# Folding the first modulation into the QKV weights of a fused adaLN, windowed-attention and GEGLU kernel

## The chip, the cores and the metric

One NeuronCore of a Trainium2 chip runs the whole kernel. Its engines run side by side, each through an instruction list of its own: TensorE (PE, with PEld for its weight loads), VectorE (DVE), ScalarE (ACT), GpSimd (POOL) and SyncE (SP), which here issues nearly all DMAs. They wait for each other through semaphores. The metric is the device time of one execution in microseconds (us).

## The reference

`x` has 2048 rows of 512; all matrices are bf16. `c` is one conditioning row, from which six vectors of 512 are made.

```python
mod = (silu(c) @ w_mod).reshape(1, 6, 1, -1)          # sa, ca, ga, sb, cb, gb
h = layernorm(x) * (1 + ca) + sa
q, k, v = split(h @ wqkv)                             # 32 heads of 16
logits = einsum(q, k at positions s, s-2, ..., s-14) * 16 ** -0.5
o = softmax(logits) @ (v at the same 8 positions)
x = x + ga * (o @ wo)
h = layernorm(x) * (1 + cb) + sb
x = x + gb * ((gelu(h @ w_gate) * (h @ w_up)) @ w_down)      # inner size 1792
```

Since the modulation acts on the columns of the normalised row `xn`, `h @ wqkv = xn @ (diag(1 + ca) wqkv) + sa @ wqkv`.

## The kernel before, in words

The rows are cut into four groups of 512 (`sg` 0 to 3), each of four chunks of 128 rows. For each group the kernel does the following:

- The first layernorm (`norm`, `norm_act`): DVE takes statistics (`bn_stats`, L394) of some chunks, ACT of the others (L377, L383), POOL raises the variance to the power -0.5 (L425), and DVE writes the normalised rows `xn` (L434).
- A transposition to `hT` (columns on partitions). Group 0 is transposed by PE in halves (`transp0`, L471). Groups 1 and 2 are transposed by PE, 16 matmuls of 128x128 against the identity (`transp`, L448), and ACT applies `1 + ca` and `sa` while it copies the result out of PSUM (`transp_ev`, L486). Group 3 is transposed by one DMA of SP (L454), and ACT applies the modulation in place.
- The projections (`qkv`, L553): twelve units of four 128x512 matmuls, one for each of q, k, v and each quarter `j` of the columns. ACT copies each out of PSUM (`qkv_ev`, L567 to L571). The PSUM pool `mm` has four buffers, so that a unit waits until the unit four places earlier has been copied out.
- The logits: DVE multiplies q with eight shifted views of k (`pq`, L616, 128x4096 elements, four for each group; group sg's are called pq sg.0 to sg.3 here), and PE sums over the 16 elements of a head with a 0/1 matrix (`LTp`, L630, 8 matmuls that use 32 columns of the array each, for each `pq`). A softmax on DVE and ACT follows.
- The values: `v` is stored to DRAM (`vscr`, L590) and loaded back in windows (`V`, L598). Its tile `vT` has one buffer; POOL copies the last 16 columns of the group before into its head (`vhalo`, L579, from `vh`, L586). DVE multiplies with the probabilities (`pv`, L705), PE sums (`o_ps`, L719), then the output projection (`x_ps`, L740) and the residual (L749). `pq` and `pv` share four buffers (`prod`).
- The second layernorm of the group, and the gated FFN: `g_ps` and `u_ps` (L770) and `y_ps` (L782).

The vectors ga, sb, cb, gb are made by PE (`gR_ps`, L343) and taken through DRAM. Fifteen matmuls on zeros (L202) at the start keep PE running before there is work.

The order of the instructions on all engines is written out by hand: every generator below is a thread, the list `ORDER` names the thread whose next operation is issued, and each engine works through its operations in that order, without overtaking. The numbers with which `Op` objects are made (0.865 and the like) don't set anything on the chip.

Of the kernel before, what the change touches and what calls it, by code (L numbers as in the profile page):

```python
# [104 lines left out]
def kernel(  # L105
# [798 lines left out]
```

## Time and profile before

| | |
|---|---|
| median of 3 runs | 235.75 us (235.43 to 236.03) |
| the profiled execution's own time | 235.66 us |
| its span, first to last instruction | 233.9 us |
| PE busy | 229.1 us, 1382 matmuls |
| DVE busy | 168.2 us |
| ACT busy | 152.5 us |
| POOL busy | 24.3 us |
| granted TensorE clock, mean | 1.000 |

The span lies 1.8 us below the execution's own time, which also holds what goes before the first and after the last instruction. A view by time (the timeline) gives start and duration of merged instructions; in brackets stands how long the engine had been idle, and who released it. Neighbouring instructions of an engine overlap at their ends, so that the distance between starts, and not the printed duration, is what one more instruction costs an engine in a dense stretch. The chain of waits follows the last instruction back to what it waited for.

### The profile page before, as it was taken

To read this page: it belongs to the slowest core of one execution; us is meant where nothing else is said; L and a number is where in the kernel's file an instruction comes from. 1 tells how busy PE (TensorE), PEld (TensorE's weight loads), DVE (VectorE), ACT (ScalarE), POOL (GpSimd) and SP (SyncE) were. 2 spreads that over 40 slices of the span, in tenths; PEclk is the share of its full clock that TensorE was granted. 3 is DMA by queue.
4 is the path that set the end of the run, shared out by engine and by line. 5 is a ranking of instruction groups with operands and counts; after the bars stand their busy time and mean duration, and the time that the engine had idled before them with its cause. 6 is when DMAs were issued, how large, how long until landed. Compare 5 with 4: busy or idle time off the path is not lost.

```text
span 233.9 us, 3653 instructions
## 1 busy us (share of the span) xinstructions
PE 229.1 (98%) x1382; PEld 106.9 (46%) x1382; DVE 168.2 (72%) x240; ACT 152.5 (65%) x284; POOL 24.3 (10%) x37
## 2 busy tenths in 40 slices
PE   7899999999999999999999999999999999999995
PEld 2755454444544344444444444444444444444443
DVE  4889999999998999999899996944852213222222
ACT  4999998877997579936786961634468631467400
POOL 3210320791200000100000010000100000000000
PEclk9999999999999999999999999999999999999999
DMA  6999776999188582045003616110023000100011
GB/s 212 386 348 241 218 301 154 266 367 396 41 266 227 209 291 82 1 92 157 22 0 100 273 45 122 38 45 0 0 47 69 0 22 22 44 4 0 0 48 45
DMA packets 30217, 30.42 MB, mean 130 GB/s; under 512 B 14840, under 2 KB 26104, under 8 KB 30200
## 3 DMA queue, kind: packets, MB, share of 16 engines
q1 hardware_dynamic: 29664, 29.67, 40.8%
q10 hardware_dynamic: 536, 0.53, 0.6%
q8 instruction: 11, 0.18, 0.3%
q14 instruction: 6, 0.05, 0.1%
HBM read 22.78 MB, written 5.31 MB: 120 GB/s over the span
## 4 chain that ended last, share of the span: by engine, by line
PE 84%; DVE 9%; DMA 3%; ACT 1%; SPq 1%; issue 0%
PE g_ps L770 21%; PE u_ps L770 21%; PE y_ps L782 19%; PE qkv_ps L553 9%; PE x_ps L740 6%; DVE pq L616 5%; PE o_ps L719 3%; DMA x<-in_A_x_dram 3%; PE LTp L630 2%; PE y_ps L793 1%; DVE xn L434 1%; DVE st L394 1%; ACT qT L567 1%; DVE e L674 1%; DVE LTp L653 1%; DVE mx L647 1%
## 5 line engine op out<-in xcount | busy, mean ns | idle before, releaser
L770 PE MATMUL g_ps<-h,Wg 128*128 128x512 bf16 x224 | 57.5, 379 | 0.0
L770 PE MATMUL u_ps<-h,Wu 128*128 128x512 bf16 x224 | 57.5, 379 | 0.0
L820 DVE TENSOR_TENSOR hht<-gl,ub 128x512 bf16<-128x512 bf16 x56 | 23.0, 420 | 33.7 <-ACT ub L809 33.5
L782 PE MATMUL y_ps<-Wd,hht 128*128 128x512 bf16 x210 | 47.0, 379 | 0.0
L809 ACT CAST ub<-u_ps 128x512 bf16<-128x512 f32 x56 | 32.9, 588 | 20.4 <-PE u_ps L770 20.4
L802 ACT ACTIVATE gl<-g_ps 128x512 bf16<-128x512 f32 x56 | 33.6, 600 | 18.4 <-PE g_ps L770 16.9
L553 PE MATMUL qkv_ps<-hT,wqkv 128*128 128x512 bf16 x184 | 42.2, 380 | 0.0
L616 DVE TENSOR_TENSOR pq<-qT,kT 128x4096 bf16<-128x4096 bf16 x16 | 36.2, 2282 | 0.6 <-ACT kT L569 0.3
L705 DVE TENSOR_TENSOR pv<-PT,V 128x4096 bf16<-128x4096 bf16 x16 | 35.8, 2282 | 0.0
L770 PEld LDWEIGHTS <-Wu 128*128 128x128 bf16 x224 | 21.7, 98 | 27.0 <-issue 1.3
L770 PEld LDWEIGHTS <-Wg 128*128 128x128 bf16 x224 | 21.7, 98 | 27.0 <-issue 1.3
L782 PEld LDWEIGHTS <-hht 128*128 128x128 bf16 x210 | 20.4, 98 | 25.0 <-issue 0.4
L553 PEld LDWEIGHTS <-wqkv 128*128 128x128 bf16 x184 | 20.1, 114 | 18.5 <-issue 2.3
L425 POOL TENSOR_TENSOR rstd<-rstd,neghalf 128x4 f32<-128x4 f32 (+1 forms) x9 | 8.7, 971 | 124.4 <-DVE rstd L414 74.7
L827 DVE TENSOR_TENSOR ot<-y_ps,x 128x512 bf16<-128x512 f32 x15 | 10.1, 686 | 13.2 <-PE y_ps L782 13.2
L749 DVE TENSOR_TENSOR x<-x_ps,x 128x512 bf16<-128x512 f32 x16 | 10.7, 684 | 6.9 <-PE x_ps L740 6.9
L740 PE MATMUL x_ps<-woP,oT 128*128 128x512 bf16 x64 | 15.3, 379 | 0.0
L730 ACT CAST oT<-o_ps 128x512 bf16<-128x512 f32 x16 | 9.2, 593 | 8.7 <-PE o_ps L719 8.7
L394 DVE BATCH_NORM_STATS2 st<-x 128x6 f32<-128x512 bf16 x19 | 12.6, 680 | 2.7 <-DMA x<-in_A_x_dram 2.6
L486 ACT ACTIVATE h<-h,modT,scl 128x512 bf16<-128x512 bf16 x12 | 9.0, 809 | 7.7 <-DMA h<-xn 7.7
L586 POOL COPY vh<-vT 128x64 bf16<-128x64 bf16 x3 | 11.7, 3899 | 14.5 <-ACT vT L571 14.5
L377 ACT ACTIVATE gl<-x 128x512 bf16<-128x512 bf16 x13 | 8.3, 645 | 4.7 <-DVE x L749 3.0
(78 smaller groups left out, 189.6 us busy)
## 6 DMA issues: line engine op xcount, KB each, us to landing
V<-vscr SPq DMA_DIRECT2D x16, 526.0 KB, 6.8
wm<-in_w_mod_dram SPq DMA_DIRECT2D x5, 512.0 KB, 8.6
vscr<-vT SPq DMA_DIRECT2D x4, 528.0 KB, 9.5
out_dram<-ot SPq DMA_DIRECT2D x15, 128.0 KB, 1.7
Wg<-in_B_w_gate_dram SPq DMA_DIRECT2D x1, 1792.0 KB
Wu<-in_B_w_up_dram SPq DMA_DIRECT2D x1, 1792.0 KB
wqkv<-in_A_wqkv_dram SPq DMA_DIRECT2D x3, 512.0 KB, 7.3
x<-in_A_x_dram SPq DMA_DIRECT2D x3, 512.0 KB, 7.4
```

Source lines behind the costliest of these rows:

```text
L394: nc.vector.bn_stats(out=k["st", c4][:], in_=src()[:, c4, :])
L553: nc.tensor.matmul(ps[:], lhsT=wqkv[blk][:, dt, j::4], rhs=B["hT", sg][:, :, dt, :], start=(dt == 0), stop=(dt == DT - 1))
L586: yield Op("POOL", 0.2, lambda: nc.gpsimd.tensor_copy(out=vh[:], in_=B["vT", sg][:, :, SG:VR]), after=[f"qkv.{sg}.2.3"], fire=f"vh.{sg}")
L616: nc.vector.tensor_tensor(out=pq[:], in0=_ap(B["qT", sg][:, j, :], [[0, W], [1, SG]]), in1=_ap(kT[:, j, sg * SG + 2:sg * SG + 2 + SG], [[2 ...
L705: nc.vector.tensor_tensor(out=t[:], in0=_ap(B["PT", sg][:, 0, :], [[SG, 2], [0, 4], [1, SG]]), in1=_ap(v[:, j, 0, :], [[8, 2], [VR, 4], [1 ...
L740: nc.tensor.matmul(ps[:], lhsT=B["oT", sg][:, j, c4 * P:(c4 + 1) * P], rhs=woP[:, j, :], start=(j == 0), stop=(j == 3))
L749: nc.vector.tensor_tensor(out=x[:, c4, :], in0=B["x1ps", sg, c4][:], in1=x[:, c4, :], op=ALU.add)
L770: nc.tensor.matmul(ps[:], lhsT=Wt[:, dt, ft * P:(ft + 1) * P], rhs=B["h2T", sg][:, :, dt, :], start=(dt == 0), stop=(dt == DT - 1))
L782: nc.tensor.matmul(ps[:], lhsT=B["hh", sg, ft][:, c4 * P:(c4 + 1) * P], rhs=B["Wd", ft // 4][:, ft % 4, :], start=(ft == 0), stop=(ft == F ...
L802: nc.scalar.activation(out=gl[:], in_=B["g", sg, ft][:], func=ACT.Gelu_apprx_tanh)
L809: nc.scalar.copy(out=ub[:], in_=B["u", sg, ft][:])
L820: nc.vector.tensor_tensor(out=hh[:], in0=B["gl", sg, ft][:], in1=B["ub", sg, ft][:], op=ALU.mult)
```

## The change

The shift and scale of the first modulation leave the row side for groups 1 to 3.

- Twelve scaled weight tiles `wq` of 128x512 are made: `wqkv` times `1 + ca`, which is a scalar on each partition. POOL makes eight (all four of q, two of k, two of v), ACT four (`WENG`). They lie in twelve of the sixteen buffers `hh` that later hold the FFN's products.
- The shift becomes a bias `sa @ wqkv`: 48 matmuls on PE of 128 columns each (`bR_ps`, L382, of the same shape as `gR_ps`), one copy by ACT (L388), a store to DRAM and a load `bC` (L392, L396). ACT adds it while it copies the projections of groups 1 to 3 out of PSUM (L623), now with an ACTIVATE of function Identity in place of a CAST.
- Groups 1 to 3 are transposed by DMA (L502). The 32 PE transposes and the 12 ACT modulations of these groups go.
- Group 0 keeps its old path and the plain weights.
- The loads of `w_down` wait for the bias and the scaled weights, and no longer for the projections of all groups.
- `ORDER` is another list.

```diff
+    WENG = {(0, 0): "POOL", (0, 1): "POOL", (0, 2): "POOL", (0, 3): "POOL", (1, 0): "POOL", (1, 1): "POOL",
+            (1, 2): "ACT", (1, 3): "ACT", (2, 0): "POOL", (2, 1): "POOL", (2, 2): "ACT", (2, 3): "ACT"}
+
+    def wqscale(eng):
...
+                    if eng == "ACT":
+                        nc.scalar.activation(out=w[:], in_=wqkv[blk][:, dt, :], func=ACT.Copy, scale=scl[:, dt:dt + 1])
+                    else:
+                        e = nc.gpsimd if eng == "POOL" else nc.vector
+                        e.tensor_scalar_mul(out=w[:], in0=wqkv[blk][:, dt, :], scalar1=scl[:, dt:dt + 1])
+                yield Op(eng, 0.6, f, after=[f"wqkv{blk}", "mod1"], fire=f"wq.{blk}.{dt}")
+
+    def qkv_bias():
...
+            for blk in range(3):
+                for kt in range(4):
+                    for ch in range(4):
+                        nc.tensor.matmul(ps[H * ch:H * ch + H, blk, :], lhsT=B["shB"][:, kt, :],
+                                         rhs=wqkv[blk][:, kt, ch * P:(ch + 1) * P],
+                                         start=(kt == 0), stop=(kt == 3), tile_position=(0, H * ch))
...
+            nc.sync.dma_start(out=bscr.rearrange("b (c n) -> c b n", n=P), in_=B["bS"][0:P:H, :, :])
...
+            nc.sync.dma_start(out=bC[:], in_=bass.AP(bscr.tensor, bscr.offset, [[4, P], [D, 3], [1, 4]]))
...
-    BY_PE = ("LN1.1", "LN1.2", "LN2.0")
+    BY_PE = ("LN2.0",)
...
-                    nc.tensor.matmul(ps[:], lhsT=wqkv[blk][:, dt, j::4], rhs=B["hT", sg][:, :, dt, :],
+                    w = B["wq", blk, dt] if sg else wqkv[blk][:, dt, :]
+                    nc.tensor.matmul(ps[:], lhsT=w[:, j::4], rhs=B["hT", sg][:, :, dt, :],
...
+                if sg:
+                    nc.scalar.activation(out=o, in_=ps[:], func=ACT.Identity, bias=bC[:, blk, j:j + 1])
+                else:
+                    nc.scalar.copy(out=o, in_=ps[:])
...
-                     ... ("h1", lambda q: ln1_ev(q) if q else ln1_ev0(False)), ("qkv", qkv),
+                     ... ("h1", lambda q: iter(()) if q else ln1_ev0(False)), ("qkv", qkv),
```

What the order does to the engines is shown at three places. On PE, whose rows are long runs of equal instructions, it is told in words. Before: PE ran the ten last units of group 0's projections, with the 16 transposes of group 1 between them, then LTp 0.0, `gR_ps`, LTp 0.1, three units of group 1, LTp 0.2, LTp 0.3. Now: the same ten units, with the 48 bias matmuls after the second of them, LTp 0.0 ahead of the last, then LTp 0.1, `gR_ps`, LTp 0.2, two units of group 1, LTp 0.3, `gR_ps`, and then 19 units of groups 1 and 2 in one piece. The changes between 32-column matmuls and full ones number the same in the whole program (16 runs of 32-column matmuls before and now).

SP, before, from the load of the last group of `x` (`vscr` is the store of `v`, `V` its load in windows, `gB` the vector ga, `escr` the softmax's probabilities):

```order
L216 DMA x<-in_A_x_dram 128x4x512
L590 DMA vscr_108<-vT 128x2112
L223 DMA wm<-in_w_mod_dram 128x4x512
L297 DMA gscr_112<-gR 4x128
L598 DMA V_563<-vscr_108 128x1x2104
L302 DMA gB<-gscr_112 128x512
L598 DMA V_563<-vscr_108 128x1x2104 x2
L590 DMA vscr_109<-vT 128x2112
L297 DMA gscr_113<-gR 4x128
L686 DMA escr_116<-e 128x1024
```

SP, now, behind that load, the store of the bias and one load of `wm`:

```order
L502 DMA_TRANSPOSE hT<-xn 128x16x128
L396 DMA bC<-bscr 128x3x4
L225 DMA wm<-in_w_mod_dram 128x4x512
L644 DMA vscr_108<-vT 128x2112
L299 DMA gscr_112<-gR 4x128
L225 DMA wm<-in_w_mod_dram 128x4x512
L652 DMA V_664<-vscr_108 128x1x2104 x2
L502 DMA_TRANSPOSE hT<-xn 128x16x128
L299 DMA gscr_113<-gR 4x128
L740 DMA escr_117<-e 128x1024
L644 DMA vscr_109<-vT 128x2112
L304 DMA gB<-gscr_112 128x512
```

The two transpositions, which wait for `xn` of groups 1 and 2, stand ahead of the stores of `v` of groups 0 and 1 and of the loads of `V`; group 1's store (`vscr_109`) has moved behind the store of the probabilities of group 0 (`escr`), and the load of `gB` behind both.

POOL, before, from the powers of group 0's layernorm to that of group 2's:

```order
L425 TENSOR_TENSOR rstd<-rstd,neghalf 128x2 x2
L425 TENSOR_TENSOR rstd<-rstd,neghalf 128x4
L586 COPY vh<-vT 128x64
L579 COPY vT<-vh 128x4x16
L425 TENSOR_TENSOR rstd<-rstd,neghalf 128x4
```

POOL, now, in the same stretch:

```order
L473 TENSOR_TENSOR rstd<-rstd,neghalf 128x2 x2
L367 TENSOR_SCALAR wq<-wqkv_137,scl 128x512 x2
L196 MEMSET kT 128x4x16
L367 TENSOR_SCALAR wq<-wqkv_137,scl 128x512 x2
L367 TENSOR_SCALAR wq<-wqkv_138,scl 128x512
L473 TENSOR_TENSOR rstd<-rstd,neghalf 128x4
L367 TENSOR_SCALAR wq<-wqkv_138,scl 128x512
L367 TENSOR_SCALAR wq<-wqkv_139,scl 128x512 x2
L640 COPY vh<-vT 128x64
L473 TENSOR_TENSOR rstd<-rstd,neghalf 128x4
L633 COPY vT<-vh 128x4x16
```

Eight scaled tiles stand around the power of group 1's layernorm, and the clearing of the first columns of `kT`, which pq 0.0 reads, has moved behind two of them.

DVE, before, from pq 0.0 to pq 0.3:

```order
L616 TENSOR_TENSOR pq<-qT,kT 128x4096
L434 TENSOR_SCALAR xn<-x,mv,rstd 128x512
L394 BN_STATS st<-x 128x6
L434 TENSOR_SCALAR xn<-x,mv,rstd 128x512 x2
L434 TENSOR_SCALAR xn<-x,sums,rstd 128x512
L616 TENSOR_TENSOR pq<-qT,kT 128x4096
L394 BN_STATS st<-x 128x6
L616 TENSOR_TENSOR pq<-qT,kT 128x4096 x2
```

DVE, now, over the same instructions:

```order
L670 TENSOR_TENSOR pq<-qT,kT 128x4096
L442 BN_STATS st<-x 128x6
L482 TENSOR_SCALAR xn<-x,mv,rstd 128x512
L442 BN_STATS st<-x 128x6
L482 TENSOR_SCALAR xn<-x,mv,rstd 128x512 x2
L482 TENSOR_SCALAR xn<-x,sums,rstd 128x512
L670 TENSOR_TENSOR pq<-qT,kT 128x4096 x2
L448 BN_AGGR mv<-st 128x2 x2
L670 TENSOR_TENSOR pq<-qT,kT 128x4096
```

One `BN_STATS` has moved ahead of the `xn` of group 1, and two `BN_AGGR` ahead of pq 0.3; the sum of DVE's work is the same.

More of the change, by code (lines that the diff above doesn't have):

```diff
@@ L275, in ffn_q @@
             for b in range(4):
[L276 removed]
+                yield Op("SP", 0.65, ldwd(b), fire=f"Wd{b}", lat=mb(0.5 if b < 3 else 0.25), after=[f"qp.0.{blk}.3" for blk in range(3)] + ["mpb"] + [f"wq.{blk}.{dt}" for blk in range(3) for dt in range(DT)])
         return act_q(), sp_q(), wm_q(), ffn_q()
@@ new lines, in qkv_bias, with f @@
+    def qkv_bias():
+        def f():
+            B["shB"] = T("hh", [P, 4, H], BF16, "shB")
+            nc.scalar.copy(out=B["shB"][:], in_=_ap(modT[:, 0:4], [[1, 4], [0, H]]))
+        yield Op("ACT", 0.25, f, after=["mod0"], take=[SL["hh"]], fire="shB")
+        def f():
+            ps = T("mm", [P, 3, P], F32, "bR_ps")
+            B["bR"] = ps
+            for blk in range(3):
+                for kt in range(4):
[3 more added lines that the diff above has]
+                                         start=(kt == 0), stop=(kt == 3), tile_position=(0, H * ch))
+        yield Op("PE", 0.64, f, quad=True, after=["shB", "wqkv0", "wqkv1", "wqkv2"], take=[SL["mm"]], give=[SL["hh"]], fire="mpb")
+        def f():
+            B["bS"] = T("ot4", [P, 3, P], F32, "bR")
+            nc.scalar.copy(out=B["bS"][:], in_=B["bR"][:])
+        yield Op("ACT", 0.4, f, after=["mpb"], take=[SL["ot4"]], give=[SL["mm"]], fire="gcb")
+        def f():
+            nc.sync.dma_start(out=bscr.rearrange("b (c n) -> c b n", n=P), in_=B["bS"][0:P:H, :, :])
+        yield Op("SP", 0.65, f, after=["gcb"], give=[SL["ot4"]], fire="bst", lat=0.3)
+        def f():
+            nc.sync.dma_start(out=bC[:], in_=bass.AP(bscr.tensor, bscr.offset, [[4, P], [D, 3], [1, 4]]))
+        yield Op("SP", 0.65, f, after=["bst"], fire="bC", lat=0.5)
@@ L556, in qkv @@
             tk = [SL["q"]] if (blk, j) == (0, 0) else []
-            yield Op("PE", 0.865, f, after=[f"LN1.{sg}.h{d}" for d in (("0.1", "1.0", "3.1") if sg == 0 else (2, 3))] + [f"wqkv{blk}"], take=[SL["mm"]] + tk,
-                     give=[SL["hT"]] if last else [], fire=f"qp.{sg}.{blk}.{j}")
+            yield Op("PE", 0.865, f, after=([f"LN1.0.h{d}" for d in ("0.1", "1.0", "3.1")] + [f"wqkv{blk}"]
+                                               if sg == 0 else [f"LN1.{sg}.t"] + [f"wq.{blk}.{dt}" for dt in range(DT)]),
+                     take=[SL["mm"]] + tk, give=[SL["hT"]] + ([SL["hh"]] * 12 if sg == NSG - 1 else []) if last else [], fire=f"qp.{sg}.{blk}.{j}")
     def qkv_ev(sg):
@@ L860 @@
         pl.spawn(mods_g(b, before))
+    for blk in range(3):
+        for dt in range(DT):
+            SL["hh"].n -= 1
+            B["wq", blk, dt] = T("hh", [P, SG], BF16, "wq")
+    for e in ("POOL", "ACT", "DVE"):
+        pl.spawn(wqscale(e))
+    pl.spawn(qkv_bias())
     for n, g in (("wds", wdscale), ("wos", woscale)):
```

18 lines of the change are left out of this document (12 added, 6 removed), and 68 rows, old and new, of the table ORDER.

## The prediction

> **What bounds the kernel now.** I read the page's busy table first, then the chain of waits in order of time, then the timelines of PE, DVE, POOL and SP up to 66 us, where every edit lies.
>
> ```profile
> PE 229.1 (98%) x1382; PEld 106.9 (46%) x1382; DVE 168.2 (72%) x240; ACT 152.5 (65%) x284; POOL 24.3 (10%) x37
> PE 84%; DVE 9%; DMA 3%; ACT 1%; SPq 1%; issue 0%
> ```
>
> PE is busy for 98% of the span and carries 84% of the chain. So PE work that goes should come off the end, unless PE then waits. The chain tells where it would wait:
>
> ```profile
> 13.68 2.29 DVE pq L616
> 15.97 0.32 DVE xn L434
> 16.29 0.60 DVE st L394
> 16.89 0.96 DVE xn L434 x3
> 17.85 2.20 DVE pq L616
> ...
> 20.66 4.40 DVE pq L616 x2
> 25.06 0.09 DVE mv L400
> ...
> 29.03 0.94 DVE xn L434 x3
> ...
> 35.60 0.62 PE LTp L630 x8
> 36.22 7.89 PE qkv_ps L553 x36
> ...
> 44.65 0.43 PE LTp L630 x8
> ...
> 61.64 0.34 PE gR_ps L343 x16
> 61.97 1.00 PE hTp L448 x16
> ...
> 65.56 0.86 PE g_ps L770 x4
> ```
>
> From 13.68 to 35.6 us the chain is DVE's, without a gap; from there it is PE's to the end. PE is dense in DVE's stretch too, but only just: its timeline has one wait, for pq 0.3, and no other.
>
> ```profile
> 17.71 0.61 PE L448 MATMUL hTp<-ident,xn 128*128 128x128 bf16 x8
> 18.16 1.03 PE L553 MATMUL qkv_ps<-hT,wqkv 128*128 128x512 bf16 x4
> ...
> 20.42 0.61 PE L630 MATMUL LTp<-pq,Mph 128*32 128x512 bf16 x8
> ...
> 25.12 0.61 PE L630 MATMUL LTp<-pq,Mph 128*32 128x512 bf16 x8 [0.16 <-DVE pq L616]
> ```
>
> At 25.12 PE has caught up with DVE. Whatever is saved on PE before that point is lost in this wait, and only what is saved behind it counts. That is the hinge of my sum.
>
> **The sum.** It is made against the profiled execution (span 233.9, own time 235.66 us, 0.09 below the median 235.75).
>
> Removed on PE: 32 transposes. Eight take 0.45 (17.71 to 18.16), so group 1's and group 2's cost 0.9 each. Added on PE: 48 matmuls of the shape of `gR_ps`, of which 16 take 0.34, so 1.0. Both the bias and group 1's transposes lie before 25.12, so neither is counted at the end; their cover is the wait for pq 0.2 and 0.3, and if DVE came earlier, the bias would cost its 1.0.
>
> When pq 0.3 ends now: 13.68 + 2.29, then st 0.60, xn 0.32, st 0.60, three xn 0.96, gives 18.45; two pq 4.40 give 22.85; two mv of 0.09 and one pq 2.20 give 25.23. That is 0.17 later than before (25.06). PE is there before: at 20.42 it had done all of group 0's units and both parts of group 1's transposition. Less 0.9 for these, plus 1.0 for the bias, plus LTp 0.0 and 0.1 (0.43 each), `gR_ps` (0.34) and 0.2 to 0.3 for the changes between kinds, its work ahead of LTp 0.2 ends near 21.9 to 22.0. So PE waits about 0.9 us for pq 0.2 (22.85), and then two units (1.73) and an LTp with its changes (0.65) fill the time to 25.23.
>
> Behind LTp 0.3, up to the `hTp` of the second layernorm at 61.97: before, 36.85 us from 25.12. Now 0.9 less (group 2's transposes), 0.86 more (two instead of three units of group 1 lie before the hinge), and two runs of 32-column matmuls fewer (six instead of eight, since `gR_ps` and `LTp` are joined). A change into and out of such a run costs about 0.22: LTp x8 take 0.62 where a run begins (35.60) against 0.43 inside one (44.65), and the 36 matmuls behind it 7.89 against 36 of 0.216 = 7.78. So 36.85 - 0.9 + 0.86 - 0.44 = 36.37, and `hTp` starts at 25.3 + 36.37, about 61.65, 0.3 earlier. It needs the `xn` of that layernorm:
>
> ```profile
> 60.66 0.72 DVE L434 TENSOR_SCALAR xn<-x,mv,rstd 128x512 bf16<-128x512 bf16 x2
> ```
>
> which ended at 61.38 and comes about 0.15 later now, 61.55; so 0.3 is nearly all that this end lets through. Behind the first `g_ps` (65.56) both programs hold the same PE work, in as many runs, so nothing is won or lost there. The sum is 235.75 - 0.3 = 235.45, say 235.5.
>
> **What that takes as free, with bounds.** First the transpositions:
>
> ```profile
> 100.19 1.96 SPq L454 DMA_TRANSPOSE h<-xn  x1
> 104.50 2.93 ACT L486 ACTIVATE h<-h,modT,scl 128x512 bf16<-128x512 bf16 x4 [2.15 <-DMA h<-xn]
> hT<-xn SPq DMA_TRANSPOSE x1, 4.4
> ```
>
> The one at 100.19 was awaited and had landed by 104.50. Group 1's `xn` ends at 18.45, so `hT` lands at 22.85, 4.4 later; PE wants it behind LTp 0.2, at 23.4. Group 2's `xn` ended at 29.97 and ends at about 30.2 now (0.17 for pq 0.3, the rest for its place), so it lands at 34.6; PE, past LTp 0.3 and a `gR_ps` at 26.2, has ten units of group 1 (8.65) to do and wants it at 34.9. Both come 0.3 to 0.5 us in time. If the landing were counted from the end of the issue (1.96 more), they would be 1.4 and 1.7 late. I take zero, by the landing row, which holds the issue. Queued behind the first on SP are the bias load and the store of group 0's `v`. A load in small pieces lands in 6.5:
>
> ```profile
> modc<-gscr SPq DMA_DIRECT2D x2, 1.0 KB, 6.5
> 10.90 1.55 ACT L567 CAST qT<-qkv_ps 128x512 bf16<-128x512 f32 x3
> L486 ACT ACTIVATE hT<-hTp,modT,scl 128x512 bf16<-128x512 bf16 x8 | 6.1, 853 | 0.0
> L383 ACT ACTIVATE gl<-x,sums 128x512 bf16<-128x512 bf16 x13 | 9.7, 750 | 0.1
> ```
>
> `bC` is issued at 20.5 and so lands at 27.0. Between the first `kT` copy at 13.7 and the first biased copy, ACT's order has eight copies of 0.48 (the row at 10.90), the copy of the bias, four scaled tiles and nine statistics instructions of 0.6 to 0.75, some 13 us in all: the biased copy is due at about 26.5. It waits 0.5 for `bC`, and PE, with four `mm` buffers, asks for that buffer at 27.1: free by this row, with 3 us on it if `bC` came as late as twice the row. ACT loses 6.1 us of modulations for groups 1 and 2 alone; it is not on the chain, and its spare time shortens nothing.
>
> POOL's scaled tiles have no row. From its rows:
>
> ```profile
> 1.07 0.29 POOL masks.py:199 TENSOR_SCALAR_AFFINE_SELECT ident<-ident 128x128 bf16<-128x128 bf16 x1
> 1.63 0.21 POOL L185 TENSOR_SCALAR_AFFINE_SELECT Mph<-Mph 128x32 bf16<-128x32 bf16 x1
> 60.08 0.37 POOL L309 TENSOR_SCALAR scl<-modc 128x4 f32<-128x4 bf16 x1
> 13.43 1.01 POOL L425 TENSOR_TENSOR rstd<-rstd,neghalf 128x4 f32<-128x4 f32 x1 [5.86 <-DVE rstd L419]
> ```
>
> 96 columns more cost 0.08, so 512 columns take 0.61 by the first two rows and 0.37 + 0.42 = 0.79 by the third. I take 0.65, nearer the two rows with 32 and 128 columns than the one with 4. Five take 3.3 us and the clearing of `kT` 0.14, of the 5.86 that POOL idled before the power at 13.43 (its row's bracket): free with 2.4 us of room for the weights to land. The three others run from 15.97, when pq 0.0 has ended, to 17.9. The first of these that PE wants is k's, at 24.3. Why they must wait for pq:
>
> ```profile
> 24.41 0.75 POOL L579 COPY vT<-vh 128x64 bf16<-128x64 bf16 x1 [3.69 <-DMA vscr<-vT]
> 30.33 0.24 POOL L586 COPY vh<-vT 128x64 bf16<-128x64 bf16 x1 [1.84 <-ACT vT L571]
> 35.07 0.57 POOL L579 COPY vT<-vh 128x64 bf16<-128x64 bf16 x1 [1.87 <-DMA vscr<-vT]
> 35.47 0.41 DVE L434 TENSOR_SCALAR xn<-x,mv,rstd 128x512 bf16<-128x512 bf16 x1
> 42.27 11.22 POOL L586 COPY vh<-vT 128x64 bf16<-128x64 bf16 x1 [6.63 <-ACT vT L571]
> 40.10 8.88 DVE L705 TENSOR_TENSOR pv<-PT,V 128x4096 bf16<-128x4096 bf16 x4
> 48.91 4.48 DVE L616 TENSOR_TENSOR pq<-qT,kT 128x4096 bf16<-128x4096 bf16 x2
> ```
>
> A copy takes 0.24 alone; the one begun at 42.27 ended at 53.49, when the unbroken line of pv and pq had ended (53.39), and those at 24.41 and 35.07 end just behind a pq. So POOL stands still during pq and pv. The Trainium skill, page "SBUF — State Buffer", section "Who interferes with whom", says that DVE and GpSimd share a port pair, and that whoever comes first holds it for the whole instruction while the other fully blocks. By that rule a scaled tile also holds DVE out, and the time would be the first rival's. What happens to DVE beside a long POOL instruction no row shows; the bounds are zero and two scaled tiles, 1.3. I take zero, since the xn at 35.47, beside the end of the copy, took 0.41, where two in a row take 0.72 (60.66); no other row is nearer.
>
> **The rivals.** *DVE is held up by POOL, or the transpositions land late.* The three scaled tiles from 15.97 on stand beside four xn and the start of pq 0.1. If two of them each hold DVE for 0.65, pq 0.3 and LTp 0.3 come 1.3 later and the hinge with them: 235.5 + 1.1 = 236.6; a transposition 1.5 late gives the same. For it: margins of 0.3 to 0.5 at both transpositions, and 0.4 at the power. Against it: the landing rows agree within 0.1.
>
> *The halo copy is shut out.* This ends clearly slower.
>
> ```profile
> 30.27 0.33 SPq L590 DMA_DIRECT2D vscr<-vT  x1
> ```
>
> Group 1's store landed at 35.07, 4.8 after its issue, and the copy into group 2's `vT` slipped in between two pq. Now the store is issued behind the probabilities, at 33.9, and lands at 38.7; DVE leaves a gap (three xn) from 38.2 to 39.2, and then woP and pv run unbroken. If the store lands after 39.2, POOL stands still, ACT waits for it with group 2's `vT`, PE runs out of `mm` buffers at 40.1, and DVE itself stops at 44.8 for want of a `prod` buffer; only then the copy runs. PE would lose 5.5 us: about 240.7. It decides at 0.5 us of lateness. Against it: `gB`, which woP waits for, is issued behind that store.
>
> *The whole PE saving comes through*: 1.8 - 1.0 and the 0.16 wait, 235.75 - 0.9 = 234.85. It needs DVE to reach pq 0.3 and the second `xn` 0.6 earlier, for which I see nothing but waits that this profile hides.
>
> **How the numbers follow.** About 0.7 us (0.3%) is what a measurement here can tell from no change. Forecast, within 0.3%: 0.47, with 235.1 to 236.4 as its own range. The whole saving: 0.20. First rival, with late landings of more than 0.9: 0.26. Halo copy: 0.07. So faster 0.20, same 0.47, slower 0.33. The range 234.8 to 237.6 leaves out the halo case and the worst of the late landings.
>
> **What would show it.** Right: PE idle near 22 us for pq L670 of about 0.9; LTp 0.3 near 25.3; `hTp` near 61.7 and the first `g_ps` near 65.3; no wait of PE behind that. Wrong: scaled tiles on POOL of well over 0.8 (the power of group 1 late, and xn behind it), xn or pq starting late beside L367, PE waiting for the DMA of `hT` near 23.4 or 34.9, ACT waiting for `bC`, or L633 lasting several us near 39.

## The result, and the profile after

The changed kernel takes 243.35 us (median of 4 runs, 242.56 to 244.59) against 235.82 us before (235.43 to 236.03). The ratio is 1.030, 95% interval 1.025 to 1.036: 7.5 us slower, where 235.5 was predicted. The profiled execution took 242.68 us, with a span of 240.6 (233.9 before). Its page:

```profile
PE 230.7 (96%) x1386; PEld 106.2 (44%) x1398; DVE 169.7 (71%) x240; ACT 148.8 (62%) x276; POOL 36.2 (15%) x45
...
PEclk9999589999999999999999999999999999999999
...
PE 84%; POOL 4%; ACT 4%; DVE 3%; DMA 3%; issue 1%; SPq 1%; ACTq 0%; POOLq 0%
...
L367 POOL TENSOR_SCALAR wq<-wqkv,scl 128x512 bf16<-128x512 bf16 x8 | 17.4, 2196 | 2.1 <-ACT hT L552 2.1
```

Three things are new. POOL stands on the chain with 4%, where it had no share at all. A scaled tile takes 2196 ns on POOL in the mean; the prediction had 650. And PE's granted clock, full in every slice before, falls to 0.5 in the slice from 24 us (a slice is 6 us). POOL's timeline of the changed kernel (start, duration, operation, count; in brackets the idle time ahead and what ended it):

```profile
9.64 3.12 POOL L367 TENSOR_SCALAR wq<-wqkv,scl 128x512 bf16<-128x512 bf16 x2 [2.10 <-ACT hT L552]
...
12.83 5.81 POOL L367 TENSOR_SCALAR wq<-wqkv,scl 128x512 bf16<-128x512 bf16 x3
18.61 1.04 POOL L473 TENSOR_TENSOR rstd<-rstd,neghalf 128x4 f32<-128x4 f32 x1
19.64 8.52 POOL L367 TENSOR_SCALAR wq<-wqkv,scl 128x512 bf16<-128x512 bf16 x3
```

The first two take 1.56 us each, with no pq of DVE beside them. Five of them and the clearing of `kT` last until 18.6, so the power of group 1 (L473) starts 5.2 us later than before (13.43); 0.4 of that is a later start of this execution (in experiment 2 the same five tiles begin at 9.20 and the power at 18.18). DVE needs its result. Its timeline now, and the start of pq 0.1 before:

```profile
14.46 2.74 DVE L670 TENSOR_TENSOR pq<-qT,kT 128x4096 bf16<-128x4096 bf16 x1 [0.39 <-POOL wq L367]
...
19.68 0.79 DVE L482 TENSOR_SCALAR xn<-x,mv,rstd 128x512 bf16<-128x512 bf16 x1 [1.87 <-POOL rstd L473]
...
22.33 4.48 DVE L670 TENSOR_TENSOR pq<-qT,kT 128x4096 bf16<-128x4096 bf16 x2
...
26.89 2.53 DVE L670 TENSOR_TENSOR pq<-qT,kT 128x4096 bf16<-128x4096 bf16 x1
```

```profile
17.77 2.28 DVE L616 TENSOR_TENSOR pq<-qT,kT 128x4096 bf16<-128x4096 bf16 x1
```

The xn of group 1 stands ahead of pq 0.1 on DVE, so pq 0.1 starts at 22.33 instead of 17.77, and pq 0.3 ends at 29.42 instead of 25.06: 4.4 us late. Now PE, which multiplies what pq leaves:

```profile
24.66 0.61 PE L684 MATMUL LTp<-pq,Mph 128*32 128x512 bf16 x8 [2.20 <-DVE pq L670]
...
26.86 1.04 PE L684 MATMUL LTp<-pq,Mph 128*32 128x512 bf16 x8 [1.26 <-DVE pq L670]
27.84 3.60 PE L602 MATMUL qkv_ps<-hT,wq 128*128 128x512 bf16 x8
31.37 0.94 PE L684 MATMUL LTp<-pq,Mph 128*32 128x512 bf16 x8
...
68.09 1.07 PE L496 MATMUL hTp<-ident,xn 128*128 128x128 bf16 x16
```

PE waits 2.20 and 1.26 us for pq, and then eight matmuls take 3.60 us, which at full clock take 1.92 by the same view (1.73 from start to start). So LTp 0.3 starts at 31.37, 2 us after pq 0.3 is done and 6.25 later than before (25.12). The clock is seen in stretches (length, busy time of PE, PEld, DVE, ACT and POOL with their counts, granted clock, DMA share, GB/s):

```profile
25.00:26.00 1.00, 0.60 (x24) 0.31 (x13) 1.00 (x1) 0.35 (x2) 1.00 (x1) 0.63 1.17 212
```

```profile
26.00:32.00 6.00, 5.14 (x24) 1.46 (x27) 4.21 (x7) 4.04 (x11) 4.56 (x4) 0.50 0.85 252
```

A mean of 0.63 from 25 to 26 us, with 1.00 before and 0.50 behind, puts the fall at 25.3: 0.6 us after the wait of 2.20 ended (24.66), and ahead of the wait of 1.26 (25.60 to 26.86). So the first wait alone brought it on. The clock is full again at 32.1, 6.8 us later.

From LTp 0.3 on nothing more is lost but the rest of the slow clock: `hTp` starts 6.2 us late, the span ends 6.7 late, most of the last half microsecond in one wait of PE for ACT in the gate stage. The chain of waits in order of time says it in five pieces (start, duration, what):

```profile
12.86 5.78 POOL wq L367 x3
18.64 1.02 POOL rstd L473
...
22.41 4.42 DVE pq L670 x2
...
26.86 1.04 PE LTp L684 x8
27.91 3.54 PE qkv_ps L602 x8
```

### The profile page after: what moved, and what is told of

Same layout as the page of the kernel before. It is cut to its first block, busy times and chain, and to the rows that moved or that the text cites. A ratio compares the mean times of both kernels' runs of the same rounds, so it can differ in the third digit from the quotient of the medians.

```text
span 240.6 us, 3687 instructions
## 1 busy us (share of the span) xinstructions
PE 230.7 (96%) x1386; PEld 106.2 (44%) x1398; DVE 169.7 (71%) x240; ACT 148.8 (62%) x276; POOL 36.2 (15%) x45
## 3 DMA queue, kind: packets, MB, share of 16 engines
q1 hardware_dynamic: 34240, 30.73, 43.3%
## 4 chain that ended last, share of the span: by engine, by line
PE 84%; POOL 4%; ACT 4%; DVE 3%; DMA 3%; issue 1%; SPq 1%; ACTq 0%; POOLq 0%
PE g_ps L824 20%; PE u_ps L824 20%; PE y_ps L836 19%; PE qkv_ps L602 12%; PE x_ps L794 6%; POOL wq L367 4%; PE LTp L684 3%; PE o_ps L773 3%; DMA wqkv<-in_A_wqkv_dram 3%; DVE pq L670 2%; PE y_ps L847 1%; ACT h L534 1%; DVE xn L482 1%; ACT qT L623 1%; ACT kT L623 1%
## 5 line engine op out<-in xcount | busy, mean ns | idle before, releaser
L874 DVE TENSOR_TENSOR hht<-gl,ub 128x512 bf16<-128x512 bf16 x56 | 23.2, 421 | 36.9 <-ACT ub L863 32.1
L836 PE MATMUL y_ps<-Wd,hht 128*128 128x512 bf16 x203 | 46.4, 379 | 0.5 <-issue 0.2
L670 DVE TENSOR_TENSOR pq<-qT,kT 128x4096 bf16<-128x4096 bf16 x16 | 37.0, 2329 | 1.4 <-PE LTp L684 1.0
L602 PE MATMUL qkv_ps<-hT,wq 128*128 128x512 bf16 x144 | 34.2, 394 | 0.0
L473 POOL TENSOR_TENSOR rstd<-rstd,neghalf 128x4 f32<-128x4 f32 (+1 forms) x9 | 8.8, 984 | 115.4 <-DVE rstd L462 68.3
L602 PEld LDWEIGHTS <-wq 128*128 128x128 bf16 x144 | 16.1, 116 | 17.0 <-issue 3.4
L367 POOL TENSOR_SCALAR wq<-wqkv,scl 128x512 bf16<-128x512 bf16 x8 | 17.4, 2196 | 2.1 <-ACT hT L552 2.1
L684 PE MATMUL LTp<-pq,Mph 128*32 128x512 bf16 x128 | 9.8, 408 | 3.5 <-DVE pq L670 3.5
```

Of the source, the lines that this page charges most:

```text
L367: e.tensor_scalar_mul(out=w[:], in0=wqkv[blk][:, dt, :], scalar1=scl[:, dt:dt + 1])
L602: nc.tensor.matmul(ps[:], lhsT=w[:, j::4], rhs=B["hT", sg][:, :, dt, :], start=(dt == 0), stop=(dt == DT - 1))
L670: nc.vector.tensor_tensor(out=pq[:], in0=_ap(B["qT", sg][:, j, :], [[0, W], [1, SG]]), in1=_ap(kT[:, j, sg * SG + 2:sg * SG + 2 + SG], [[2 ...
L684: nc.tensor.matmul(B["LT", sg][H * g:H * g + H, 4 * t:4 * t + 4, :], lhsT=M[:], rhs=B["pq", sg, j][:, 4 * t:4 * t + 4, g * P:(g + 1) * P], ...
L836: nc.tensor.matmul(ps[:], lhsT=B["hh", sg, ft][:, c4 * P:(c4 + 1) * P], rhs=B["Wd", ft // 4][:, ft % 4, :], start=(ft == 0), stop=(ft == F ...
L874: nc.vector.tensor_tensor(out=hh[:], in0=B["gl", sg, ft][:], in1=B["ub", sg, ft][:], op=ALU.mult)
```

## The experiments

The theory that I set out with: POOL's tiles are two to three times as dear as taken, the power behind them is late, and PE's waits then let its clock drop. The rivals: the transpositions by DMA, the bias load or the halo copy are late. Ratios are to the kernel before in the same comparison, with 95% intervals. Edits are shown shortened, changes of `ORDER` as the order that they give on an engine.

| | kernel | median us | ratio |
|---|---|---|---|
| 1 | changed, POOL's tiles not made | 239.79 | 1.0137 (1.0104 to 1.0169) |
| 2 | changed, PE kept busy | 241.44 | 1.0220 (1.0187 to 1.0252) |
| 3 | changed, power first | 242.04 | 1.0252 (1.0209 to 1.0295) |
| 4 | before, with POOL's tiles | 242.77 | 1.0286 (1.0238 to 1.0333) |
| 5 | 1, one w_mod load earlier | 238.72 | 1.0100 (1.0066 to 1.0134) |
| 6 | 1, V's loads later | 240.27 | 1.0151 (1.0095 to 1.0207) |
| 7 | 5 and 6 together | 241.99 | 1.0230 (1.0177 to 1.0283) |
| 8 | before, POOL price list | 238.53 | one run |
| 9 | 1, three loads much earlier | 240.88 | 1.0181 (1.0131 to 1.0232) |
| 10 | changed, loads as in 9 | 242.94 | 1.0268 (1.0209 to 1.0328) |
| 11 | 5, woP's loads later | 240.52 | 1.0185 (1.0149 to 1.0221) |
| 12 | 5, woP's loads on POOL's queue | 240.87 | 1.0189 (1.0148 to 1.0230) |
| 13 | 5, woP's loads last | 239.24 | 1.0144 (1.0127 to 1.0161) |
| 14 | 11, group 2 transposed by PE | 237.62 | 1.0084 (1.0051 to 1.0116) |

**1. Without POOL's eight tiles.**

```diff
 w = B["wq", blk, dt]
+if eng == "POOL":
+    return
...
-w = B["wq", blk, dt] if sg else wqkv[blk][:, dt, :]
+a = WENG[blk, dt] == "ACT"
+w = B["wq", blk if a else 1, dt if a else 2 + dt % 2] if sg else wqkv[blk][:, dt, :]
```

> The changed kernel without POOL's eight scaled tiles (their scaling is left out; the four that ACT makes are read in their place, so PE, DVE, ACT and all DMAs do the same work). POOL theory (the tiles' 1.56 us each hold back group 1's power, and with it DVE's xn and pq): the power stands near 13.4 us again instead of 18.6, LTp 0.3 ends near 25.8, the first g_ps stands near 65.3, no slice of the clock row under 9 behind 24 us, and the time is 234.8 to 236.5 us, what the prediction made of the change with tiles that are hidden. Rival (late DMA transposes, the bias load, or the halo copy): 241 to 244, since none of these is touched. Rival (POOL and something else, half each): 238 to 240.

239.79 us: without the tiles' work 3.6 of the 7.5 us are gone, about half. The power is back in time on POOL's timeline, and LTp 0.3 stands at 25.94 on PE's:

```profile
13.70 1.01 POOL L474 TENSOR_TENSOR rstd<-rstd,neghalf 128x4 f32<-128x4 f32 x1 [6.01 <-DVE rstd L468]
```

```profile
25.94 0.61 PE L685 MATMUL LTp<-pq,Mph 128*32 128x512 bf16 x8
27.75 0.41 PE L344 MATMUL gR_ps<-wm,scB 128*32 128x128 bf16 x16 [1.19 <-ACT qT L624]
...
38.38 7.96 PE L603 MATMUL qkv_ps<-hT,wq 128*128 128x512 bf16 x36 [1.47 <-DMA hT<-xn]
```

Two new waits stand behind it, 1.19 and 1.47 us. The first is put down to ACT, but the weight load of the same `gR_ps` waited 1.7 us for a w_mod block: its load stands behind group 1's transposition on SP's queue and was issued at 22.70. The second is group 2's transposition, 7.6 us from issue (30.73) to landing. Neither shows in the changed kernel, where all that they meet is later and group 2's transposition lands in 4.8 us. So the third outcome of the expectation, half each, is the one that came.

**2. PE kept busy where it waited.**

```diff
+for n in (9, 5):        # ahead of LTp 0.1 and of LTp 0.2
+    t = T("att", [P, SG], F32, "busy_ps")
+    for k in range(n):
+        nc.tensor.matmul(t[:], lhsT=gB[:, 0:P], rhs=gB[:], start=True, stop=True)
```

> The changed kernel with 14 idle matmuls of 128x512 on PE (nine ahead of LTp 0.1, five ahead of LTp 0.2, some 3 us, into a PSUM tile that nothing reads), where PE waited 2.20 and 1.26 us for DVE's pq. POOL's part is untouched. Clock theory (a part of the loss is PE at half clock from 26.9 to 32.3 us, set off by those waits): the eight qkv matmuls behind LTp 0.2 take 1.73 us instead of 3.60, the clock row keeps its 9s between 24 and 36 us, and the time falls by 2.0 to 2.6 us to 240.8 to 241.4. If the slow matmuls are slow for another reason (wq not yet there, SBUF shared with POOL): 243.3, or 0.2 to 0.5 more for the added matmuls.

```profile
26.98 1.92 PE L610 MATMUL qkv_ps<-hT,wq 128*128 128x512 bf16 x8
...
40.54 7.96 PE L610 MATMUL qkv_ps<-hT,wq 128*128 128x512 bf16 x36 [1.32 <-DMA hT<-xn]
```

More work, and 1.9 us less time (241.44 against 243.35): the eight matmuls run at full clock. The clock drop is a cause of its own. Between the two profiled executions LTp 0.3 follows LTp 0.2 after 2.62 us instead of 4.51, again 1.9; but PE, earlier now, meets the late transposition of group 2 (1.32), and their times differ by 0.8 only (241.89 against 242.68, 0.4 of it the start).

**3. The power ahead of the third tile.**

```diff
-POOL: wq x2, clear kT, wq x3, power of group 1, wq x3
+POOL: wq x2, clear kT, power of group 1, wq x6
```

> The changed kernel with group 1's power ahead of the third of POOL's eight tiles instead of behind the fifth; no work added or left out. POOL theory: the power stands near 13.4 us and group 1's xn are not late, LTp 0.2 and 0.3 come some 4 us earlier than in the changed kernel; but the last six tiles (1.56 each, 9.4 us, and shut out while pq runs) end near 27 to 30 us instead of 28.1, and PE's first units of group 1 wait for them: 236.5 to 241 us, with PE's wait put down to POOL's wq and no longer to pq. If the time hangs on POOL's total and not on the power's place: 243. If tiles and pq can run side by side, the tiles end near 24.5 and the time is 235.5 to 236.

The power starts at 14.03 and the xn are in time, but the six tiles behind it take 2.5 us each beside pq, and PE waits for them. POOL's timeline, then PE's:

```profile
15.07 15.22 POOL L366 TENSOR_SCALAR wq<-wqkv,scl 128x512 bf16<-128x512 bf16 x6
```

```profile
24.67 0.61 PE L683 MATMUL LTp<-pq,Mph 128*32 128x512 bf16 x8 [1.57 <-DVE pq L669]
...
30.34 18.07 PE L601 MATMUL qkv_ps<-hT,wq 128*128 128x512 bf16 x75 [1.14 <-POOL wq L366]
```

242.04 us is 1 above the range: the tiles also stretched DVE (the pair of pq took 4.89 instead of 4.49), and the clock fell here too (0.88 and 0.87 in the stretches from 26 to 32 and to 40 us). POOL's total is too long at either place of the power that was tried; the tiles, not the power's place, are what to be rid of.

**4. The tiles alone, in the kernel before.**

```diff
+for n in range(8):      # five ahead of group 1's power on POOL, three behind
+    nc.gpsimd.tensor_scalar_mul(out=dum, in0=wqkv[n // 4 if n < 6 else 2][:, n % 4, :],
+                                scalar1=scl[:, n % 4:n % 4 + 1])
```

> The kernel before, with eight scaled tiles of the same kind made on POOL around group 1's power (five ahead, three behind) into a tile that nothing reads: the tiles alone, without the rest of the change. POOL theory: the power of group 1 moves from 13.4 to 17.5 to 18.7 us, DVE's xn, pq and PE's LTp behind it go late by 4 to 5 us, the clock drops as in the changed kernel, and the time is 240 to 244 us (without the clock drop 238.5 to 241). Rivals (transposes by DMA, bias load, halo copy): 235.8 to 236.5.

POOL's timeline, then DVE's:

```profile
9.06 10.11 POOL L354 TENSOR_SCALAR dum<-wqkv,scl 128x512 bf16<-128x512 bf16 x5 [1.45 <-ACT hT L510]
```

```profile
20.21 0.79 DVE L440 TENSOR_SCALAR xn<-x,mv,rstd 128x512 bf16<-128x512 bf16 x1 [4.13 <-POOL rstd L431]
```

Eight POOL instructions whose result nobody reads cost 6.6 us (242.77 against 236.20). With no folded weights, no DMA transposes and no bias this is nearly the whole loss of the change. Five tiles took 10.11 us: 5 x 1.56, and the 2.29 of the pq that ran beside them.

**5. The w_mod load ahead of group 1's transposition.**

```diff
-SP: ..., w_mod 2, transpose group 1, bC, w_mod 3, ...
+SP: ..., w_mod 2, w_mod 3, transpose group 1, bC, ...
```

> The first experiment's kernel (changed, without POOL's eight tiles; their scaling is left out) with one load moved on SP's queue: the w_mod block that gR_ps needs, which stood behind group 1's transposition and bC, is issued ahead of that transposition. Queue theory (a transposition holds SP for 2 to 5 us, so what is queued behind it is late): PE's wait of 1.19 us in front of gR_ps at 27.75 goes. But hT of group 2 landed at 38.34 and still does, so PE waits there 2.4 to 2.7 us instead of 1.47, and the time stays within 0.5 us of 239.8. If the late w_mod block was the only thing that counted: 238.6. If the earlier load crowds out the transposition (hT of group 1 later than 23.9): 240.3 to 241.

SP's queue, then PE:

```profile
18.98 4.29 SPq L503 DMA_TRANSPOSE hT<-xn  x1
...
31.95 1.79 SPq L503 DMA_TRANSPOSE hT<-xn  x1
```

```profile
25.31 1.92 PE L603 MATMUL qkv_ps<-hT,wq 128*128 128x512 bf16 x8 [1.29 <-DMA hT<-xn]
```

238.72, 1.1 us less than in 1; 239.8 was expected. The wait for w_mod is gone, and a wait of 1.29 for group 1's transposition has come, behind 1 MB of w_mod loads. But group 2's landed in 4.7 us here and was not awaited, which I had not expected. The time is that of the second outcome (238.6), by another sum.

**6. V's loads behind group 2's transposition.**

```diff
-SP: ..., V x2, transpose group 2, ...
+SP: ..., transpose group 2, V x2, ...
```

> The first experiment's kernel (scaling of eight tiles left out) with two loads of group 0's V moved on SP's queue from in front of group 2's transposition to behind it. Contention theory (the transposition took 7.6 us from issue to landing instead of 4.4 because the two loads of 526 KB each were under way): it is issued near 30.7 and lands by 35.2 to 36, ahead of PE's need at 36.9; the wait of 1.47 us goes, and the time is 238.2 to 238.6 us. V is wanted near 44 and comes by 42, so nothing is paid for it. Rival (the transposition is slow by itself, from its size or its place): it lands at 37.5 to 38.3 still, 239.3 to 239.8 us.

```profile
42.92 2.75 PE L603 MATMUL qkv_ps<-hT,wq 128*128 128x512 bf16 x12 [0.81 <-ACT vT L624]
```

Group 2's transposition was not awaited, as expected: PE went on with its result about 5.6 us after the issue (the trace holds no landing for it; the 5.0 that a view gives is group 1's). But V's loads then ran ahead of the store of group 1's `v`; the halo copy on POOL waited for that store until 42.20, ACT, which writes the same `vT`, stood for 2.8 us until then, PE for ACT, and group 3's transposition was late as well (0.97). The time did not fall (240.27): "nothing is paid for it" was wrong.

**7. Both moves.** The edit is that of 5 and of 6.

> Both moves of the two kernels above together (scaling of eight tiles left out). If the two waits of PE, 1.19 and 1.47 us, are what the transpositions cost through SP's queue, both go: hTp of the second layernorm stands near 62.7, and the time is 236.9 to 237.5 us. What then remains against the kernel before, 1 us, is LTp 0.3, 0.8 us later (0.3 from the start of pq 0.0, the rest from ACT). If ACT or the bias load holds PE as soon as the two waits are gone: 238 to 239. If the transposition stays slow without the V loads in front: 239 or above.

241.99: a clear miss. The profiled execution is one whose opening loads came late, PE's first work waiting for them:

```profile
8.39 0.55 PE L286 MATMUL modT_ps<-scT,wm 128*128 128x1 bf16 x16 [2.17 <-DMA wm<-in_w_mod_dram]
...
46.12 4.44 PE L603 MATMUL qkv_ps<-hT,wq 128*128 128x512 bf16 x12 [2.15 <-ACT vT L624]
```

After that the clock was 0.50 from 10 to 12 us and pq 0.0 stood at 16.92. The loads that I moved are issued later than that. Further on the wait of 6 is back: the halo copy stands at 45.40, PE waits 2.15 us for ACT, and the twelve matmuls behind take 4.44 instead of 2.75, the clock having fallen once more (46.4 to 49.8). So moving V's loads costs here too. The other five runs (241.5 to 242.4) had full clock, and no profile shows where their time went, so what the two moves give together stays open.

**8. A price list of POOL.**

```diff
+for n in (32, 128, 256, 512):     # each twice
+    nc.gpsimd.tensor_scalar_mul(out=d[:, 0:n], in0=gB[:, 0:n], scalar1=scl[:, 0:1])
+for n in (32, 128, 256, 512):
+    nc.gpsimd.tensor_copy(out=d[:, 0:n], in_=gB[:, 0:n])
+for n in (128, 512):
+    nc.gpsimd.tensor_scalar_mul(out=d[:, 0:n], in0=gB[:, 0:n], scalar1=1.5)
```

> The kernel before with POOL instructions into a tile that nothing reads, near 170 us, where POOL and mostly DVE are idle: tensor_scalar by a column of scl on 128x32, 128x128, 128x256 and 128x512 bf16, copies of the same sizes, and tensor_scalar by a constant on 128x128 and 128x512, twice each. If the price is proportional to the elements (3.0 ns a column, from the 1.56 us of the changed kernel): 0.10 to 0.2, 0.4, 0.8 and 1.56 us. If it is 0.37 and 0.83 ns a column, as the prediction had it from the affine_selects: 0.4, 0.47, 0.58, 0.79, and the 1.56 us has another reason (weights just landing, DVE beside it). Constant instead of column: the same if the scalar's fetch isn't what costs. Copies: 0.24 at 64 columns, 1.3 or below at 512.

```profile
173.24 0.41 POOL L355 TENSOR_SCALAR dum<-gB,scl 128x32 bf16<-128x32 bf16 x1
173.74 0.60 POOL L354 TENSOR_SCALAR dum<-gB,scl 128x128 bf16<-128x128 bf16 x1
...
176.33 0.93 POOL L355 TENSOR_SCALAR dum<-gB,scl 128x256 bf16<-128x256 bf16 x1
...
179.01 1.56 POOL L355 TENSOR_SCALAR dum<-gB,scl 128x512 bf16<-128x512 bf16 x1
...
183.79 0.62 POOL L360 COPY dum<-gB 128x512 bf16<-128x512 bf16 x1
...
187.44 1.49 POOL L363 TENSOR_SCALAR dum<-gB 128x512 bf16<-128x512 bf16 x1
```

From 256 to 512 columns the multiplication costs 0.63, that is 2.5 ns a column; the copy takes 0.62 at 512 where the multiplication takes 1.56. A constant instead of a column of scalars saves 0.07. So the 1.56 is the price of the operation, not of fresh weights or of DVE beside it, and both lines of the expectation were off: there is a fixed 0.3 and then three times the slope of the affine_selects.

**9. Three loads much earlier, woP's later.**

```diff
-SP: x2, woP x4, x3, bscr, w_mod 2, transpose group 1, bC, ..., w_mod 3, ..., w_mod 4, V x2, ...
+SP: x2, x3, w_mod 2, w_mod 3, bscr, transpose group 1, bC, ..., w_mod 4, woP x4, V x2, ...
```

> The first experiment's kernel (POOL's eight tiles not made, their scaling left out) with loads moved on SP's queue so that the first transposition meets less traffic: x of group 3 and two w_mod blocks right behind x of group 2, near 8 us as the kernel before has its w_mod blocks, and the four loads of woP behind the third w_mod block, near 25 us. V's loads stay where they were. Theory (what is left of the loss without POOL's tiles is load traffic around the transpositions): group 1's hT lands by 23.9, PE waits for no w_mod block and for hT of group 2 at most 0.5 us, hTp of the second layernorm stands near 62.5, and the time is 236.3 to 237.3 us. Rival (bias, biased copies, or ACT's order cost as much by themselves): hTp at 64 or later, 238 to 239.5. If the prediction's sum holds once nothing is late: 235.5.

```profile
8.06 0.55 PE L286 MATMUL modT_ps<-scT,wm 128*128 128x1 bf16 x16 [1.40 <-DMA wm<-in_w_mod_dram]
...
39.80 7.96 PE L603 MATMUL qkv_ps<-hT,wq 128*128 128x512 bf16 x36 [1.75 <-DMA hT<-xn]
```

240.88, a miss. Group 1's transposition was in time, group 2's was not. And this execution has the late start too: PE waits 1.40 us for a w_mod block, the clock is 0.50 from 10 to 12 us, pq 0.0 stands at 16.76. All six runs have a mean clock of 0.991 to 0.993, so probably all have it; three of the eleven runs of the kernel before beside them (238.6 to 240.2, clock 0.986 to 0.993) look like it. Whether the moved loads bring it on is open; the block awaited had landed before the first of them was issued.

**10. The same loads in the whole changed kernel.** The edit of 9, in the changed kernel.

> The changed kernel whole, POOL's eight tiles included, with the loads moved as in the kernel beside it. Theory (POOL's tiles hold back group 1's power whatever the loads do): the power stays near 18.6 us, LTp 0.2 near 26.9, the clock drops as in the changed kernel, and the time is 242 to 243.5 us. If the earlier x and w_mod loads crowd the qkv weights that POOL's first tile waits for: 243.5 to 245. Rival (traffic is the larger cause): under 240.

242.94, as the theory had it, though by another sum: a late start (pq 0.0 at 16.71) and no long clock drop behind it. The power ran from 18.12 to 20.33.

**11. woP's loads out of the way of group 1's transposition.**

```diff
-SP: x2, woP x4, x3, bscr, w_mod 2 and 3, transpose group 1, bC, ..., w_mod 4, V x2, ...
+SP: x2, x3, bscr, w_mod 2 and 3, transpose group 1, bC, ..., w_mod 4, woP x4, V x2, ...
```

> The first experiment's kernel (POOL's eight tiles not made, their scaling left out), with the w_mod block ahead of group 1's transposition as in the fifth experiment, and the four loads of woP (512 KB) taken from in front of that transposition to behind the third w_mod block. Traffic theory (the fifth experiment's wait of 1.29 us for group 1's hT came from what was loading ahead of it): hT lands by 24, that wait is under 0.4 us, and if group 2's transposition still lands within 5 us of its issue, hTp of the second layernorm stands near 63 and the time is 237 to 237.9 us; if the woP loads push V's and so that transposition back, 1 to 1.7 us of PE's wait come there instead and the time is 238 to 239. If the traffic ahead is not what makes a transposition late: the wait of 1.3 us stays, 238.7. A start in which the opening loads land late (pq 0.0 near 16.8 instead of 14.1) adds 2.5 us to any of these.

```profile
23.76 1.92 PE L603 MATMUL qkv_ps<-hT,wq 128*128 128x512 bf16 x8
25.63 0.62 PE L685 MATMUL LTp<-pq,Mph 128*32 128x512 bf16 x8
...
37.87 7.96 PE L603 MATMUL qkv_ps<-hT,wq 128*128 128x512 bf16 x36 [2.48 <-DMA hT<-xn]
```

The wait for group 1's transposition is gone, with the traffic ahead of it. Group 2's, issued at 30.41 behind woP's and V's loads, is awaited until 37.87. The profiled execution takes 238.87; the median is 240.52. Four of the eight runs have a mean clock of 0.993 and take 240.5 to 241.2; the other four have full clock and take 238.9 to 240.5.

**12. woP's loads from POOL.**

```diff
-nc.sync.dma_start(out=woP[H * i:H * i + H, :, :], in_=wo_v[i])
+nc.gpsimd.dma_start(out=woP[H * i:H * i + H, :, :], in_=wo_v[i])   # behind vh.0
```

> As the kernel beside it (POOL's eight tiles not made, their scaling left out), but the four loads of woP are issued from POOL, which has nothing to do there, behind its first copy near 23.4 us, so that they hold up nothing on SP's queue. Traffic theory: hT of group 1 lands by 24, V's loads and group 2's transposition are issued as early as in the fifth experiment, neither transposition is awaited for more than 0.4 us, and the time is 236.4 to 237.3 us: what the change gives at best, with its tiles free of charge and its transpositions in time. If the sum of the prediction holds for the rest: 235.5 to 236. If ACT or the bias holds PE instead: 238 or more.

```profile
37.43 9.65 PE L603 MATMUL qkv_ps<-hT,wq 128*128 128x512 bf16 x36 [1.96 <-DMA hT<-xn]
```

A miss: the transposition still lands 6.9 us after its issue, so the place of woP's loads on SP's queue is not what holds it. And the 36 matmuls behind the wait take 9.65 instead of 7.96: here a wait of 1.96 us set off the clock drop that 2.48 us did not set off in 11.

**13. woP's loads behind group 2's transposition.**

```diff
-SP: ..., w_mod 4, woP x4, V x2, transpose group 2, ...
+SP: ..., w_mod 4, V x2, transpose group 2, woP x4, ...
```

> As the eleventh experiment (POOL's eight tiles not made, their scaling left out; one w_mod block ahead of group 1's transposition), but the four loads of woP stand behind group 2's transposition on SP's queue, so that neither transposition has them ahead. Traffic theory: group 2's hT, awaited for 2.48 us there, lands within 5 us of its issue near 30.4, PE waits for it 0 to 0.4 us, hTp of the second layernorm stands near 62.2, and the profiled execution takes 236.4 to 236.9 us (with a clock drop in some runs, a median up to 237.5). If V's two loads alone are enough to hold the transposition back: a wait of 1 to 2 us, 237.7 to 238.7. If something behind it (woP scaled late, pv and with it PE) takes the place: 238 or more with PE's wait behind 47 us.

```profile
37.00 7.96 PE L603 MATMUL qkv_ps<-hT,wq 128*128 128x512 bf16 x36 [1.07 <-DMA hT<-xn]
...
47.85 0.62 PE L774 MATMUL o_ps<-pv,Mph 128*32 128x512 bf16 x8 [1.68 <-DVE pv L760]
```

Both of the rival outcomes came: without woP ahead of it the transposition was still 1.07 late, and woP, scaled late, held up pv and with it PE (1.68). That V's loads are what held the transposition is not shown: they stood ahead of it in 5 too, where it was in time. 239.24 (the profiled execution, 241.10, is the slowest of its five).

**14. Group 2 transposed by PE again.**

```diff
-BY_PE = ("LN2.0",)
+BY_PE = ("LN2.0", "LN1.2")
...
+nc.scalar.copy(out=B["hT", sg][:, :, dt, :], in_=B[("xn1", sg), dt // 2][:, :, dt % 2, :])
```

> As the eleventh experiment, but group 2's rows are transposed by PE again, as in the kernel before, and copied out by ACT without modulation (the folded weights stay). One part of the change undone: PE gets 0.9 us of transposes and 0.2 for changes of kind back, loses the wait of 2.48 us for that DMA, and ACT gets four copies, about 2.4 us. Theory (that transposition is the rest of the loss): 237.3 to 238 us without a clock drop, PE waiting for nothing between 27 and 60 us. If ACT's four copies make its biased copies late: PE waits for mm buffers near 33 to 38 us, 238.5 to 239.5. If the rest lies elsewhere: 240 or more.

```profile
26.09 0.61 PE L695 MATMUL LTp<-pq,Mph 128*32 128x512 bf16 x8
...
34.69 9.66 PE L613 MATMUL qkv_ps<-hT,wq 128*128 128x512 bf16 x44
...
63.25 1.07 PE L498 MATMUL hTp<-ident,xn 128*128 128x128 bf16 x16
```

237.62 us, within the expected range and the lowest of all variants: PE waits for nothing between 27 and 60 us. Against 11 it wins 2.9 in the median, 1.4 between the profiled executions. Against the kernel before, 11 was 4.8 behind in the median and 3.1 in the profiled execution, so group 2's transposition by DMA is about half of what was left. The profiled execution's 1.8 us against the kernel before are 1.0 up to LTp 0.3 (26.09 against 25.12), 0.4 from there to `hTp` (37.16 against 36.79 by the same view; the prediction's terms without the saving of group 2's transposes are 0.86 - 0.44), and 0.4 behind. None of the versions tried beats the kernel before, even with POOL's tiles free of charge.

## Why the prediction was wrong

**The step that failed is the price of POOL's tile.** 0.65 us stood between bounds of 0.61 and 0.79; it is 1.56 alone and 2.2 in the mean beside DVE. Both bounds came from rows of affine_select and of a 128x4 instruction, and the slope of one operation was lent to another: 0.83 ns a column there, 2.5 here. Five tiles and the clearing, 3.4 us in the prediction, ended at 18.6, and the power, free at 13.4 in it, started then. The sign that the prediction named for it, tiles well over 0.8 with the power and xn late behind them, is what the profile shows. Experiment 4 shows that this alone costs 2.9%. Without it 1.4% are left (1), from waits that the changed kernel, late already, does not show; so the two losses don't add up. There was no row of the operation beyond four columns. But the idle time of 5.86 us gives the price at which five tiles and the clearing must make the power late, (5.86 - 0.14) / 5 = 1.14 us even with all weights there at once (0.73 from 9.64, where the first tile started), and that price should have been a rival with a chance.

**The second step was missing: the clock.** The prediction has no term for what PE does after a wait. A wait of 2.20 us halved it for 6.8 us, which took in the next wait; experiment 2 gives 1.9 us for that. The Trainium skill, page "TensorE: Matmul & The Clock Gate", Part 1, describes a free-running activity window of about 3.4 us, and its section "Why this matters for your kernels" advises against idle gaps above some 3 us. The runs agree that the phase matters (1.96 us halved the clock in 12, 2.48 did not in 11); a gap shorter than the page's was enough.

**The hinge held where DVE was in time.** In 1 and 11 PE did catch up with DVE at pq 0.3, after a wait of 0.5 for pq 0.2 where 0.9 was forecast, and work saved ahead of it was lost; in the changed kernel the slow clock left PE 2 us behind there. Behind it the sum was right: 36.37 us from LTp 0.3 to `hTp` were forecast, and experiment 11 has 38.90 with a wait of 2.48 in it, so 36.42 without. The predicted 25.3 for LTp 0.3 was 25.63 there, 0.31 of it because pq 0.0 starts later (13.99), which I had taken as unmoved.

**DVE beside POOL.** Zero was taken, with bounds up to 1.3. In the changed kernel pq 0.0 took 2.74 instead of 2.29 and DVE was 1.5 us busier in all (169.7 against 168.2), so the bound was nearer than the value. By the rule cited in the prediction, that the two shut each other out, five tiles and one pq take the sum of both, and in experiment 4 they did; in 3 six tiles (9.4) and the pq beside them (9.1) went into 15.2 us, so there they overlapped in part.

**The first rival was half right.** Transpositions 1.5 us late were in it, at 1.1 us. They are not late in the changed kernel, where they landed in 4.3 and 4.8 us; group 2's is in 1, 9, 11 and 12 (1.5 to 2.5 us). The landing of 4.4 us came from a quiet moment (DMA share 0.00 from 39 to 40 us); where one is known it was 4.3 to 7.6 here. For group 1 it fell from about 6.3 to 4.3 when woP's loads were moved from in front of it (5 and 11). The list of what stands behind the first transposition on SP lacked the w_mod block, for which PE waited 1.19 in 1.

**The rest.** The bias load was in time: the first biased copy ran at 27.06 in 1 (forecast 26.5 to 27). The halo copy was not shut out: L633 took 0.24 and 0.98. Nothing was won or lost behind the first `g_ps` but 0.5 us, most of it one wait for ACT, where I had said none. Two slips in the sums of the rivals bear on nothing: 235.5 and 5.5 make 241.0, not 240.7, and 1.8 - 1.0 and 0.16 make 0.96, not 0.9.

Two things stay open: which loads make group 2's transposition land after about 7 us in 11 and 12 and after 4.7 in 5, and why the opening loads land 2 us late in some executions and in all of some builds.

## What to carry to other kernels

Price an instruction on an idle engine from a row of the same operation on the same engine, and where there is none, work out the price at which the first instruction queued behind it comes late, and give that case a chance. An engine with 5.9 us of idle time ahead of a critical instruction is not free for work without a known duration. When PE is made to wait about 2 us or more, allow for a halved clock behind the wait: it came after some such waits and not after others.

## What the runs showed of the hardware

A POOL multiplication of 128x512 bf16 by a scalar takes 1.56 us, a copy of the same tile 0.62. PE's granted clock fell to 0.50 about 0.6 us behind waits of 2.20 us (changed kernel) and 1.96 (12) and 0.3 behind one of 2.15 (7), and once in the opening behind one of 1.40 (9); it did not after one of 2.48 (11). These falls lasted 3.4 us each, but the one in the changed kernel lasted 6.8. A transposition of 512 KB by DMA holds SP's queue for 1.8 to 5.7 us and lands 4.3 to 7.6 us after its issue.
